# The idle products at the head of a Sinkhorn-attention and MoE kernel, cut from 29 wide into 113 narrow ones

## Chip, core and metric

The kernel runs on one core of a Trainium2 chip. The metric is the device time of one execution in microseconds; before the change it is 240.62 us, the median of 3 runs (240.29 to 241.72). A lower time is better. Matrix products run on TensorE (PE; its weight loads are listed apart as PEld), elementwise work on VectorE (DVE), ScalarE (ACT) and GpSimd (POOL), and transfers are issued from SyncE (SP), POOL and ACT.

## What is computed

Attention over sorted blocks, then a gated MLP. Four batches of eight heads have 768 rows of width 64, in eight blocks of 96 rows. An 8 x 8 matrix per head is normalized five times over rows and columns (Sinkhorn), the blocks of keys and values are mixed by it, each block of queries attends to its own mixed block, and the result of all heads goes through two weight matrices with x cos(x) between them:

```python
for _ in range(5):
    P = P - np.max(P, axis=-1, keepdims=True)
    P = np.exp(P)
    P = P / (np.sum(P, axis=-1, keepdims=True) + 1e-09)
    P = P / (np.sum(P, axis=-2, keepdims=True) + 1e-09)
...
k_sorted = np.einsum('bhij,bhjcd->bhicd', P, k_b)
v_sorted = np.einsum('bhij,bhjcd->bhicd', P, v_b)
scores = scale * np.matmul(q_b, k_sb.transpose(0, 1, 2, 4, 3))
attn = softmax(scores)
x = np.matmul(attn, v_sb)          # heads side by side: 3072 x 512
h = x @ w_in                       # 512 x 2048
out = (h * np.cos(h)) @ w_out      # 2048 x 512
```

## The kernel before

After a head of about 14 us the work goes by n = 0 to 7, half a batch each: scores (`S`, L1344 or L1357), row maxima (`M`), subtraction (`X`), exponentials (`E`), transposed weights (`TP` or a transposing transfer), the product with the mixed values (`AV`, L1445), normalization (`N`), a transpose (`XP`), then the first MLP product (`U`, L1505, or `U4`, L1528), the cosine (`C`), the gate (`G`) and the second MLP product (`D`, L1550). The table PLAN, written by hand, gives the order of these steps; the program keeps this order on every engine. No line of PLAN is touched by the change.

The head stands ahead of PLAN and is written out in code. On SP and POOL it starts the loads of the sort matrix P, of the first queries (`q_mem`), keys and values. VectorE and ScalarE run the five Sinkhorn rounds in turn: ScalarE takes an exponential `E` (L1172), VectorE six small operations (`normalize`, L1146 to L1151), the last of which feeds the next exponential; in the last round it writes `sorted_by`. ScalarE's queue is in order, and between the exponentials of rounds 2, 3 and 4 it copies the transposed first queries from PSUM to `q_turned` (`q_place`, L1166): head pair 0 in round 2, pair 1 in round 3, pairs 2 and 3 in round 4.

TensorE's own order in the head is:

1. 15 idle products (`keep_warm`, L1083) of a zero tile `warm` with itself: 128 x 128 weights, 512 columns, into a PSUM tile `idle` that nothing reads.
2. `q_twice(0)` and `q_twice(1)` (L1160): 16 transposes each out of `q_mem`, into `qps` tiles.
3. 2 idle products into a `big` tile.
4. In round 2: 6 idle products, then `q_twice(2)`. In round 3: 2 idle products, then `q_twice(3)`. In round 4: 4 idle products.
5. `block` (L1205) twice: 8 products each of `sorted_by` with a selection matrix. VectorE spreads them into `bd` and `bdv` (L1210), and with these PLAN's first steps mix keys (L1225) and values (L1281).

The idle products of step 4 and the `qps` and `bl` tiles share the PSUM pool `acc`, which has two buffers. A tile there may be written when the last tile in its buffer has been read (by a `q_place` copy) or, for an `idle` tile, written. Which of the two buffers a tile gets is not in the source; it is settled when the program is built. The wait itself is a semaphore of the engine that releases the buffer. Each idle product is two instructions on TensorE, a load of the weights and the product.

Further idle products in PLAN's steps (the fills of `kp` and `v0`, and one of 256 columns in `TP` and `AV` for n = 0) are called with counts and widths of their own and stay as they are.

Of the kernel before, what the change touches and what calls it, by code (L numbers as in the profile page):

```python
# [10 lines left out]
FP32 = mybir.dt.float32  # L11
# [852 lines left out]
def kernel(  # L864
# [46 lines left out]
    big = ctx.enter_context(tc.tile_pool(name="big", bufs=3, space=bass.MemoryType.PSUM))  # L911
    acc = ctx.enter_context(tc.tile_pool(name="acc", bufs=2, space=bass.MemoryType.PSUM))
# [47 lines left out]
    def load_q(n):  # L960
        b, ih = n // 2, n % 2
        if n < NQ:

            nc.gpsimd.dma_start(
                out=q_rows, in_=q[b][:, ih * IC * blk:(ih + 1) * IC * blk].rearrange(
                    "h (p r) d -> p h (r d)", r=QR))
        else:
            src = q[b].rearrange("h (i c) d -> c i h d", c=blk).rearrange(
                "c i (h e) d -> c i h e d", e=2)
            q_heads = q_zeroed(n).rearrange("p (e x) -> p e x", e=2)[:, :, :QZ].rearrange(  # L970
                "p e (i h w) -> p i h e w", i=IC, h=H2)[:, :, :, :, :D]
            for i in range(IC):
                for e in range(2):
                    nc.gpsimd.dma_start(  # L974
                        out=q_heads[:, i, :, e], in_=src[:, ih * IC + i, :, e])
# [27 lines left out]
    def load_w_in(z):  # L1003
        c = slice(z * Dff // 4, (z + 1) * Dff // 4)
        nc.gpsimd.dma_start(out=w_in_t[:, :, c], in_=w_in_d[:, :, c])
# [75 lines left out]
    def keep_warm(times, t, cols=512):  # L1081
        for _ in range(times):
            nc.tensor.matmul(  # L1083
                t[:, :cols], warm[:], warm[:, :1].to_broadcast([128, cols]),
                start=True, stop=True)

    keep_warm(15, big.tile([128, 512], FP32, name="idle", tag="big"))


    V, A = nc.vector, nc.scalar  # L1090
# [53 lines left out]
    def normalize(it, out):  # L1144

        nc.vector.reduce_sum(sums[0][:], E_eps[:], axis=AX.X)  # L1146
        nc.vector.reciprocal(over[0][:], sums[0][:])
        nc.vector.tensor_tensor(Q, E, by_row(over[0]), op=ALU.mult)
        nc.vector.reduce_sum(sums[1][:], Q_eps.rearrange("p i j -> p j i"), axis=AX.X)
        nc.vector.reciprocal(over[(1, 2, 1, 3, 1)[it]][:], sums[1][:])  # L1150
        nc.vector.tensor_tensor(out, Q, by_column(over[(1, 2, 1, 3, 1)[it]]), op=ALU.mult)  # L1151
# [3 lines left out]
    def q_twice(h2):  # L1155
        ps = turns[h2] = acc.tile([128, 2, IC, QR, blk // QR], BF16, name="qps", tag="acc")
        for hp in range(2):
            for r in range(QR):
                for x in range(2):
                    nc.tensor.transpose(  # L1160
                        ps[x * D:(x + 1) * D, hp, :, r],
                        q_rows[:, h2 * 2 + hp, r * D:(r + 1) * D], ident[:blk, :blk])

    def q_place(h2):
        dst = q_turned[0][:, :, :QW].rearrange("d e (i h c) -> d h e i c", h=H2, c=blk)
        A.copy(dst[:, h2], turns.pop(h2).rearrange("d e i r p -> d e i (r p)"))  # L1166

    def idle(times):
        keep_warm(times, acc.tile([128, 512], FP32, name="idle", tag="acc"))

    for it in range(5):
        nc.scalar.activation(E, less[:], AF.Exp)  # L1172
        if it == 0:
            nc.vector.reduce_sum(
                maskp.rearrange("p (b e x) -> p b x e", b=2, e=2),
                ident.rearrange("p (b x e j) -> p b x e j", b=2, e=2, j=nb), axis=AX.X)
            A.copy(
                order.rearrange("k (p r) -> k p r", r=QR),
                ident[:blk, :blk].rearrange("k (r p) -> k p r", r=QR))
            q_twice(0)  # L1180
            q_twice(1)
            keep_warm(2, big.tile([128, 512], FP32, name="idle", tag="big"))
        if it >= 2:
            q_place(it - 2)
            if it < 4:
                idle((6, 2)[it - 2])
                q_twice(it)
            else:
                idle(4)
                q_place(3)  # L1190
        normalize(it, (less if it < 4 else sorted_by)[:])
        if it == 1:
            nc.gpsimd.tensor_copy(held[:B * H], over[2][:, :1])
            for z in range(3):
                load_w_in(z)
        if it == 3:
            nc.gpsimd.tensor_copy(held[:B * H], over[3][:, :1])
            load_w_in(3)
            load_q(1)
# [477 lines left out]
```

## Time and profile before

| | |
|---|---|
| median of 3 runs | 240.62 us (240.29 to 241.72) |
| the profiled execution | 241.18 us |
| its span, first to last instruction | 239.1 us |
| PE busy | 227.2 us (95%) |
| DVE busy | 172.2 us (72%) |
| ACT busy | 153.1 us (64%) |
| POOL busy | 93.5 us (39%) |
| share of PE in the chain that ended last | 72% |

The span leaves 241.18 - 239.1 = 2.1 us of the execution outside. The profile lists each instruction with its start and its duration; products overlap, so the time that one takes of TensorE is read from the spacing of their starts, or from a row of the chain that holds several of them, not from the duration of one. The chain that ended last is followed back from the last instruction, at each step to what released it; a piece in it has a start, a length and a line. In a row of the timeline, what stands in brackets is how long the engine was idle ahead of it and who ended that. One of the 29 idle products has no record in this trace.

### The profile page before, as it was taken

How to read it: one execution, taken by the hardware profiler on the slowest of the kernel's cores; microseconds unless marked ns; L12 is line 12 of the kernel's file. 1: busy time of each engine (PE TensorE's matmuls, PEld its weight loads, DVE VectorE, ACT ScalarE, POOL GpSimd, SP SyncE). 2: the span in 40 equal slices, each digit the busy share in tenths (PEclk: the TensorE clock that was granted, in tenths of full speed). 3: DMA queues.
4: the chain of work that ended last, by engine and by line, in shares of the span. 5: the costliest groups of instructions: out<-in, count | busy, mean ns of one | idle time of the engine just before them, and what ended most of it. 6: DMA issues, size and time to landing. Idle time of an engine off the chain costs nothing.

```text
span 239.1 us, 5437 instructions
## 1 busy us (share of the span) xinstructions
PE 227.2 (95%) x2224; PEld 142.3 (60%) x2246; DVE 172.2 (72%) x284; ACT 153.1 (64%) x205; POOL 93.5 (39%) x117
## 2 busy tenths in 40 slices
PE   8889999999999999997999999999999899999994
PEld 2468799567666666654665456655665355455553
DVE  5658977898789677886589966996889839445610
ACT  3357966578789838873889647773675476736511
POOL 7689994895960098921708006200000000000000
PEclk9999999999999999999999999999999999999999
DMA  6999999994999999979959979844853370232012
GB/s 88 209 199 204 205 220 213 152 203 149 111 121 176 153 162 109 183 174 144 104 86 100 121 133 234 52 76 75 159 170 68 51 197 3 46 97 90 0 44 88
DMA packets 66423, 30.89 MB, mean 129 GB/s; under 512 B 55136, under 2 KB 61920, under 8 KB 66144
## 3 DMA queue, kind: packets, MB, share of 16 engines
q0 software_dynamic: 24048, 13.64, 41.8%
q1 hardware_dynamic: 42064, 16.73, 33.0%
q8 instruction: 17, 0.28, 0.5%
q10 hardware_dynamic: 288, 0.20, 0.3%
q14 instruction: 6, 0.05, 0.1%
HBM read 27.27 MB, written 6.29 MB: 140 GB/s over the span
## 4 chain that ended last, share of the span: by engine, by line
PE 72%; DMA 10%; DVE 9%; ACT 5%; issue 2%; SPq 1%; POOL 1%; ACTq 0%; POOLq 0%; DVEq 0%
PE h L1505 29%; PE o L1550 21%; DMA pT<-p_buf 5%; PE h L1528 4%; PE av L1445 3%; PE vs L1281 2%; PE sc L1344 2%; DMA vperm<-p_buf 2%; ACT p_buf L1403 2%; DMA xT<-xn 2%; DVE s L1399 2%; DVE mx L1385 1%; PE xps L1479 1%; PE o L1641 1%; PE ks L1225 1%
## 5 line engine op out<-in xcount | busy, mean ns | idle before, releaser
L1550 PE MATMUL o<-w_out_t,gg 128*128 128x512 bf16 x349 | 84.2, 379 | 1.2 <-issue 0.3
L1505 PE MATMUL h<-xT,w_in_t 128*128 128x384 bf16 x448 | 78.4, 326 | 0.4 <-DMA xT<-xn 0.4
L1517 DVE TENSOR_TENSOR gg<-c,h 128x768 bf16<-128x768 f32 x56 | 52.4, 949 | 21.3 <-ACT c L1511 21.1
L1511 ACT ACTIVATE c<-h,half_pi 128x768 f32<-128x768 f32 x56 | 50.2, 900 | 21.4 <-PE h L1505 20.4
L1505 PEld LDWEIGHTS <-w_in_t 128*128 128x128 bf16 x448 | 42.1, 98 | 26.2 <-issue 0.5
L1550 PEld LDWEIGHTS <-gg 128*128 128x128 bf16 x368 | 33.3, 98 | 33.3 <-DVE gg L1517 0.3
L1385 DVE TENSOR_REDUCE mx<-sc 96x8 f32<-96x768 f32 (+1 forms) x41 | 31.6, 771 | 4.4 <-PE sc L1344 3.4
L1403 ACT ACTIVATE p_buf<-s 96x768 bf16<-96x768 f32 x32 | 26.2, 841 | 8.7 <-DVE s L1399 5.2
L1024 POOL COPY vperm<-kv 64x1536 bf16<-64x1536 bf16 (+1 forms) x10 | 28.0, 2844 | 1.2 <-DMA kv<-in_v_dram 1.2
L1399 DVE TENSOR_TENSOR s<-sc,mx 96x384 f32<-96x384 f32 (+1 forms) x33 | 24.2, 734 | 1.6
L1457 DVE TENSOR_TENSOR xn<-av,r 96x512 bf16<-96x512 f32 x32 | 22.0, 686 | 1.1
L974 POOL DMA_DIRECT2D kv<-in_q_dram x24 | 15.9, 674 | 0.8 <-issue 0.8
L1455 DVE RECIPROCAL r<-av 96x8 f32<-96x8 f32 x32 | 6.4, 200 | 11.6 <-PE av L1445 11.4
L1094 ACT CAST kTs<-ks 128x512 bf16<-128x512 f32 (+1 forms) x17 | 10.6, 632 | 5.2 <-PE ks L1225 5.2
L1094 ACT COPY kv<-o 128x512 f32<-128x512 f32 (+2 forms) x11 | 5.9, 535 | 12.2 <-PE o L1550 9.6
L1344 PEld LDWEIGHTS <-q_turned 128*128 128x128 bf16 x168 | 9.8, 98 | 3.5 <-issue 0.4
L1344 PE MATMUL sc<-kTs,q_turned 128*128 128x96 bf16 x168 | 11.6, 206 | 0.3 <-DMA kTs<-kTs 0.3
L1083 PE MATMUL idle<-warm 128*128 128x512 bf16 x28 | 9.8, 498 | 2.1 <-ACT q_turned L1166 1.0
L1094 ACT COPY xT<-xps 128x384 bf16<-128x384 bf16 (+1 forms) x11 | 5.5, 506 | 9.0 <-PE xps L1479 9.0
L974 POOL DMA_DIRECT2D q_mem<-in_q_dram x16 | 10.7, 688 | 1.3 <-DMA kv<-in_v_dram 1.0
L1528 PE MATMUL h<-xT,w_in_t 128*128 128x192 bf16 x128 | 11.1, 246 | 0.0
L1445 PEld LDWEIGHTS <-pT 96*128 96x128 bf16 (+1 forms) x160 | 7.2, 101 | 6.0 <-DMA pT<-p_buf 4.2
(117 smaller groups left out, 264.4 us busy)
## 6 DMA issues: line engine op xcount, KB each, us to landing
out_dram<-kv SPq DMA_DIRECT2D x12, 256.0 KB, 2.6
out_dram<-o_s SPq DMA_DIRECT2D x10, 256.0 KB, 3.0
w_in_t<-in_moe_w_in_dram POOLq DMA_DIRECT2D x4, 512.0 KB, 12.0
w_out_t<-in_moe_w_out_dram POOLq DMA_DIRECT2D x4, 512.0 KB, 12.6
kv<-in_k_dram POOLq DMA_DIRECT2D x2, 768.0 KB, 10.3
kv<-in_v_dram POOLq DMA_DIRECT2D x2, 768.0 KB, 13.3
pair<-in_k_dram POOLq DMA_DIRECT2D x2, 768.0 KB, 10.9
kv<-in_v_dram POOLq DMA_DIRECT2D x6, 256.0 KB, 5.5
```

The lines of the kernel that those rows point to most:

```text
L974: nc.gpsimd.dma_start(out=q_heads[:, i, :, e], in_=src[:, ih * IC + i, :, e])
L1024: nc.gpsimd.tensor_copy(dst, src)
L1094: eng.copy(dst, src)
L1344: nc.tensor.matmul(out, q_of(n, hp)[:, x:x + 128], keys_of(n, u, h2, hp), start=True, stop=True)
L1385: nc.vector.reduce_max(mx[:], s_view(n, u, hp), axis=AX.XY if n < 2 else AX.X)
L1399: nc.vector.tensor_tensor(s, sc, mx.to_broadcast(list(s.shape)), op=ALU.subtract)
L1403: nc.scalar.activation(p[:, :, :blk], s_t.pop((n, u)).rearrange("p e h c -> p (e h) c"), AF.Exp, scale=scale)
L1457: nc.vector.tensor_tensor(xn.rearrange("p h e d -> p e h d"), avv[:, :, :, :D], r.to_broadcast([blk, 2, H2, D]), op=ALU.mult)
L1505: nc.tensor.matmul(o[:, f2, :TC], w_in_t[:, kk, f * 128:(f + 1) * 128], xT[n][:, kk], start=(kk == 0), stop=(kk == KC - 1))
L1511: nc.scalar.activation(c[:], ps["h", n, fp][:, :, :TC], AF.Sin, bias=half_pi[:, 0:1])
L1517: nc.vector.tensor_tensor(gt[n, fp // 2][:, f:f + 2], ps.pop(("c", n, fp))[:], ps.pop(("h", n, fp))[:, :, :TC], op=ALU.mult)
L1550: nc.tensor.matmul(out_ps[n, ts][:], gt[n, q][:, f % 4, ts * 128:(ts + 1) * 128], w_out_t[:, f, :], start=(f == 0), stop=(f == FC - 1))
```

## The change

Every one of the four `keep_warm` calls of the head gets more and narrower products. The 15 of 512 columns become 57 of 135; the 2 into the `big` tile become 8 of 128; `idle(6)`, `idle(2)` and `idle(4)` become 24, 8 and 16 of 128 columns. The columns are 57 x 135 = 7695 instead of 15 x 512 = 7680 at the start, and the same as before elsewhere (4 x 128 = 512). There are 113 - 29 = 84 more products, each with its load of weights.

```diff
-    keep_warm(15, big.tile([128, 512], FP32, name="idle", tag="big"))
+    keep_warm(57, big.tile([128, 512], FP32, name="idle", tag="big"), 135)
...
     def idle(times):
-        keep_warm(times, acc.tile([128, 512], FP32, name="idle", tag="acc"))
+        keep_warm(4 * times, acc.tile([128, 512], FP32, name="idle", tag="acc"), 128)
...
-            keep_warm(2, big.tile([128, 512], FP32, name="idle", tag="big"))
+            keep_warm(8, big.tile([128, 512], FP32, name="idle", tag="big"), 128)
```

The built program differs in one more thing, which the diff does not show: the `acc` tiles of the head take other buffers, and so other waits. No engine's instructions change places; TensorE has 168 more of them. On TensorE, from round 2 to round 3, before the change (in brackets the semaphore that an instruction waits for, Activation being ScalarE's; `idle_225` is the tile of `idle(6)`, `qps_232` of `q_twice(2)`, `idle_257` of `idle(2)`, `qps_260` of `q_twice(3)`):

```order
L1083 MATMUL idle_203<-warm_121 128x512
L1083 LDWEIGHTS warm_121
L1083 MATMUL idle_225<-warm_121 128x512 [waits Activation_49]
...
L1160 LDWEIGHTS q_mem_93
L1160 MATMUL qps_232<-ident_90,q_mem_93 64x4x24 [waits PE_49]
...
L1083 MATMUL idle_257<-warm_121 128x512 [waits Activation_49]
...
L1160 MATMUL qps_260<-ident_90,q_mem_93 64x4x24 [waits PE_49]
```

And the same place now (`idle_273` is the tile of `idle(6)`, now 24 products, `qps_298` of `q_twice(2)`, `idle_323` of `idle(2)`, `qps_332` of `q_twice(3)`):

```order
L1083 MATMUL idle_245<-warm_121 128x128
L1083 LDWEIGHTS warm_121
L1083 MATMUL idle_273<-warm_121 128x128 [waits Activation_49]
...
L1160 LDWEIGHTS q_mem_93
L1160 MATMUL qps_298<-ident_90,q_mem_93 64x4x24 [waits Activation_49]
...
L1083 MATMUL idle_323<-warm_121 128x128 [waits PE_49]
...
L1160 MATMUL qps_332<-ident_90,q_mem_93 64x4x24 [waits PE_49]
```

Before, `q_twice(2)` took the buffer of `idle(6)` and waited for those products on its own engine, and `idle(2)` waited for ScalarE's second `q_place`. Now `q_twice(2)` waits for that second `q_place` and `idle(2)` for the products of `idle(6)`; `q_twice(3)` waits for the products of `idle(2)` in both.

The place where the head's TensorE work meets VectorE's, the end of `idle(4)` and the first `block`, before:

```order
L1083 MATMUL idle_288<-warm_121 128x512 [waits Activation_49]
L1083 LDWEIGHTS warm_121
L1083 MATMUL idle_288<-warm_121 128x512
...
L1205 LDWEIGHTS pair_89 [waits DVE_49,Pool_49]
L1205 MATMUL bl_300<-sorted_by_156,pair_89 128x8 [waits Activation_49]
```

and now:

```order
L1083 MATMUL idle_360<-warm_121 128x128 [waits Activation_49]
L1083 LDWEIGHTS warm_121
L1083 MATMUL idle_360<-warm_121 128x128
...
L1205 LDWEIGHTS pair_89 [waits DVE_49,Pool_49]
L1205 MATMUL bl_384<-sorted_by_198,pair_89 128x8 [waits Activation_49]
```

Both wait for the same as before (`idle(4)` for ScalarE's third `q_place`, `block` for `sorted_by` and for the fourth `q_place`); 16 products stand between instead of 4.

## Prediction

> **What bounds the kernel now.** I read the page first, then the chain that ended last, then the timeline of the first 15 us.
>
> ```profile
> span 239.1 us, 5437 instructions
> PE 72%; DMA 10%; DVE 9%; ACT 5%; issue 2%; SPq 1%; POOL 1%; ACTq 0%; POOLq 0%; DVEq 0%
> ```
>
> TensorE carries most of the chain over the whole span, but the change touches only the head, and what counts there is what the chain runs through in the head. Its pieces from round 3 to the first mixed keys:
>
> ```profile
> 9.89 0.26 ACT E L1172
> ...
> 11.43 0.22 DVE less L1151
> ...
> 11.73 0.26 ACT E L1172
> 11.99 0.69 ACT q_turned L1166
> 12.68 0.04 issue
> 12.72 1.03 PE idle L1083 x4
> 13.75 0.32 PE bl L1205 x8
> 14.06 0.03 issue
> 14.09 0.30 DVE bd L1210
> 14.39 0.13 issue
> 14.51 0.64 PE ks L1225 x16
> ```
>
> Up to 11.99 us the chain is Sinkhorn alone, VectorE and ScalarE in turn; TensorE's idle products and transposes lie beside it. Only the last four idle products stand in it, between the third copy of `q_turned` and the first `block`. The timeline shows how closely:
>
> ```profile
> 7.10 0.74 PEld L1160 LDWEIGHTS <-q_mem 96*64 96x64 bf16 x32 [0.43 <-DMA q_mem<-in_q_dram]
> 9.03 1.47 PE L1083 MATMUL idle<-warm 128*128 128x512 bf16 x5 [0.52 <-ACT q_turned L1166]
> 10.05 0.77 ACT L1166 COPY q_turned<-qps 128x768 bf16<-128x768 bf16 x1
> 10.55 0.53 PE L1160 MATMUL qps<-ident,q_mem 96*64 96x96 bf16 x16
> 11.01 0.61 PE L1083 MATMUL idle<-warm 128*128 128x512 bf16 x2
> 11.68 0.53 PE L1160 MATMUL qps<-ident,q_mem 96*64 96x96 bf16 x16
> 11.90 1.46 ACT L1166 COPY q_turned<-qps 128x768 bf16<-128x768 bf16 x2
> 12.71 0.81 POOL L964 DMA_DIRECT2D q_mem<-in_q_dram x1
> 12.72 1.03 PE L1083 MATMUL idle<-warm 128*128 128x512 bf16 x4 [0.51 <-ACT q_turned L1166]
> 13.27 0.21 DVE L1151 TENSOR_TENSOR sorted_by<-Q,over 32x64 bf16<-32x64 f32 x1
> 13.68 0.58 PE L1205 MATMUL bl<-sorted_by,pair 32*128 32x8 bf16 x16
> ```
>
> `sorted_by` is done at 13.27 + 0.21 = 13.48. The chain shows 0.13 us from VectorE's `bd` to the products that use it, so `block` could start at 13.61; it starts at 13.68. The idle products therefore hold it by at most 0.07 us, and that is all that a change of them can give.
>
> **The price of a narrow product.** The rate of TensorE changes once within the first stage:
>
> ```profile
> L1083 PE MATMUL idle<-warm x5: 607/631/632, 1.0 to 2.7; 128*128 128x512 bf16 x5
> L1083 PE MATMUL idle<-warm x3: 382/432/632, 6.1 to 6.8; 128*128 128x512 bf16 x3
> L1083 PE MATMUL idle<-warm x5: 377/379/380, 9.0 to 10.1; 128*128 128x512 bf16 x5
> 5.00:6.00 1.00, 1.00 (x4) 0.29 (x2) 0.89 (x3) 0.00 (x0) 0.93 (x3) 1.00 1.85 296
> ```
>
> The first five start 1.7 / 4 = 0.43 us apart and last 631 ns; of the three from 6.1 us on the first is still slow and the last fast, so the full rate sets in near 6.6 us. The granted clock (third figure from the end of the last row) says 1.00 all the while, so the durations are what shows it. At full rate:
>
> ```profile
> 30.09 2.68 PE h L1528 x32
> 43.76 1.02 PE sc L1344 x24
> 44.78 3.45 PE o L1550 x16
> L1528 PE MATMUL h<-xT,w_in_t 128*128 128x192 bf16 x128 | 11.1, 246 | 0.0
> L1344 PE MATMUL sc<-kTs,q_turned 128*128 128x96 bf16 x168 | 11.6, 206 | 0.3 <-DMA kTs<-kTs 0.3
> L1344 PEld LDWEIGHTS <-q_turned 128*128 128x128 bf16 x168 | 9.8, 98 | 3.5 <-issue 0.4
> 15.40 0.99 PEld L1225 LDWEIGHTS <-kv 64*128 64x128 bf16 x32 [0.23 <-issue]
> ```
>
> A product of 512 columns costs 3.45 / 16 = 216 ns, one of 192 costs 2.68 / 32 = 84 ns, one of 96 costs 1.02 / 24 = 42.5 ns, each with a new load of weights that lasts 98 ns by itself. The loads are hidden at both widths. Between them, 128 columns come to 42.5 + (32 / 96) x 41.3 = 56 ns and 135 to 59 ns. Four narrow ones cost 225 ns for one wide one's 216. That price is nearest to rows of the same kind on both sides, and I take it. Its bounds: below, 216 / 4 = 54 ns; above, a load of 98 ns that isn't hidden at all.
>
> The Trainium skill has a higher price, in TensorE: Matmul & The Clock Gate, Back-to-back issue gap: a sustained stream of load and product takes about 81 ns each at 128 columns. By that the last 16 alone would take 16 x 81 = 1.30 us. The two rows above speak against it, since 96 columns take about half as much and 192 hardly more.
>
> **The parts of the change.** *The 57 at the start.* At the slow rate 135 columns take 0.43 x 135 / 512 = 0.113 us if columns alone count. By 6.6 us, 5.6 / 0.113 = 49 or 50 are through, the other 7 or 8 take 0.059 us each, and the stage ends at 7.0 to 7.1 us. Now the fifteenth starts at 6.8 and frees the array 0.22 us later, also about 7.0; the transposes then start at 7.10 and are listed as released by the transfer of `q_mem`. So nothing moves. If the loads were not hidden at the slow rate (double the 98 ns, say 0.2 us on top of each 0.113), 18 would be through by 6.6 us, the other 39 would take 59 to 157 ns each, and the transposes would start at 8.9 to 12.7 us; the first copy, wanted before the exponential at 9.89, would hold Sinkhorn by 0.2 us at the one end (done at 8.9 + 0.4 + 0.77 = 10.1) and by 4 at the other. TensorE keeping a load hidden behind 64 columns at full rate (32 loads in 0.99 us, 31 ns each) excludes nearly all of that.
>
> *The 8 in the big tile, the 24 and the 8.* They cost 17, 56 and 17 ns more and stand beside Sinkhorn. What is moved there is the wait. `q_twice(2)` starts at 10.55 now; in the change it waits for the second copy, 10.05 + 0.77 = 10.82, and with the 0.04 us from copy to product that the chain shows, starts at 10.87, though its 24 products end at 9.03 + 24 x 0.056 = 10.4. Queued behind it on TensorE: 8 idle products, from 10.87 + 0.46 = 11.33 to 11.78 (0.46 is the way from 10.55 to 11.01 now), then `q_twice(3)`, which waits until the last of them has drained, near 11.95 (a narrow product lasts 206 to 246 ns), and ends at 12.0 + 0.53 = 12.53. Who waits for these: the third copy, which can't start before 11.90 and finds its transposes done at 11.4; the fourth copy, which starts at 11.90 + 1.46 - 0.77 = 12.59 and finds them done at 12.53; and POOL's load of the next queries into `q_mem`, which has its turn at 12.71. Cover is 0.5, 0.06 and 0.18 us. The second is thin, but if the fourth copy slips, `block` still has 0.3 us to spare between its end, 11.90 + 1.46 = 13.36, and 13.68. The cost is nothing; without that cover it would be the 0.32 us of the wait.
>
> *The 16 in round 4.* They start with the third copy's end as before, 12.72, and take 16 x 0.056 = 0.90 us where four wide ones took 0.86. `block` moves from 13.68 to 13.72: **+0.04 us**, and everything behind it follows. By the bounds of the price: 0 (54 ns) to the 1.2 us worked out under the rivals.
>
> *168 more instructions on TensorE* must also be fetched:
>
> ```profile
> q8 instruction: 17, 0.28, 0.5%
> ```
>
> 0.28 MB in 17 packets is 16.5 KB each; 168 instructions against some 4,500 on TensorE is 4%, about one more packet. In the row of L1225 TensorE takes in 64 instructions in 0.99 us without a gap, and the change asks for 114 in 6 us. I take nothing; one gap of issue, 0.23 us in the bracket of that row, is the upper bound.
>
> **Sum.** 241.18 + 0.04 = 241.22 us for the profiled execution, which lies 0.56 us over the median of its kernel. On the median: 240.62 + 0.04 = 240.66, said as 240.7 us. No change.
>
> **The rivals.** *A narrow product costs its weight load.* With 98 ns each, the 24 end at 11.4, `q_twice(2)` at 11.9, the 8 at 12.6, `q_twice(3)` runs from 12.8 to 13.3, its copy ends at 14.1, and the 16 end at 14.9 instead of 13.6: +1.2 us, **241.9 us**. For it: a load's own 98 ns is longer than the 56 ns of the product. Against it: L1344 runs such pairs at 42.5 ns. With the skill's 81 ns the same steps give 14.04 for the end of the 16, and about 241.1.
>
> *The slow rate lasts.* The 57 are there to bring TensorE to its full rate, and it came 5.6 us after the first product. If short products with a load between them count for less and the rate doesn't come by 6.6 us, everything TensorE does in the head costs double. One more such interval, to 12.2 us: the 24 run from about 10.0 to 12.4, and the copies and the 16 follow from there until 14.9, +1.2 us. Two intervals, to 17.8 us: the 24 end at 12.7, `q_twice(2)` at 13.6, its copy and the 8 at 14.5, `q_twice(3)` at 15.7, the 16 at 17.5 instead of 13.6: +3.9 us, **244.5 us**, slower. It passes 1% if the slow rate holds beyond about 15 us. For it: nothing else in the head keeps TensorE so densely busy. Against it: at the slow rate 135 columns fill the array as long as 512 do, and the narrow products of L1225 with 64 columns between 14.5 and 16.5 us don't bring the slow rate back. The skill's rule (same page, What's actually happening) is that a window of time that passes busy, not a number of products, sets the rate; by it this rival falls away.
>
> *Faster.* Removing all hold on `block` gives 0.07 us, **240.55**. An earlier full rate gives nothing, since the transposes at 7.10 wait for `q_mem` anyway. I find no mechanism for a gain over 1%.
>
> **How the numbers follow.** 1% of the time is 2.4 us, about what a measurement of this kernel can tell from no change. The forecast has 0.84, the price of the load (81 or 98 ns) 0.08, the lasting slow rate 0.06 (0.05 of it long enough for over 1%), and the faster end 0.02 for what I don't see. So faster by over 1%: 0.02; within 1%: 0.93; slower: 0.05. The runs of before spread from 0.33 below their median to 1.1 above; the range takes a little more than this below, and above reaches past the load's 241.9: 239.9 to 242.0.
>
> **What would show it.** In the profile of the change: the 57 start near 0.113 us apart and then 0.059, the rate turning near 6.6 us, and `q_twice(0)` within 0.1 us of 7.10; `q_twice(2)` behind the second copy, near 10.87; its exponentials at the same distances from one another as now; 16 idle products at 56 ns from 12.72 and `block` at about 13.72; from there on all as now. Wrong would be: narrow products over 70 ns apart at full rate; products that still last over 250 ns after 9 us; or a span that differs by over 1 us with the head in place.

## The result: faster, by 0.6%, and not in the head

| | before | the change |
|---|---|---|
| median of 20 runs | 240.64 us | 239.29 us |
| all runs | 239.42 to 241.78 | 237.61 to 241.15 |
| ratio | | 0.9938 (95% interval 0.9913 to 0.9964) |
| profiled execution's span | 239.1 us | 235.7 us |

The gain lies within the 1% that the prediction called no change, but the interval of the ratio leaves out 1, and 239.29 us lies below the range that was given, 239.9 to 242.0. The two profiled executions differ by 3.4 us, more than the medians do (1.35 us); the runs of the change spread over 3.5 us and its profile is of one near their lower end. So the profile tells where the time can go, and the ratios how much.

**The head did what was predicted, from round 2 on.** The chain that ended last in the change, from the last Sinkhorn round on:

```profile
11.76 0.26 ACT E L1172
12.01 0.69 ACT q_turned L1166
12.70 0.04 issue
12.74 1.08 PE idle L1083 x16
13.82 0.52 PE bl L1205 x16
```

The 16 narrow products stand where the 4 wide ones stood, 1.08 us instead of 1.03. The timeline of TensorE there, and VectorE's `bd`:

```profile
10.90 0.53 PE L1160 MATMUL qps<-ident,q_mem 96*64 96x96 bf16 x16 [0.30 <-ACT q_turned L1166]
12.05 0.53 PE L1160 MATMUL qps<-ident,q_mem 96*64 96x96 bf16 x16
13.76 0.58 PE L1205 MATMUL bl<-sorted_by,pair 32*128 32x8 bf16 x16
14.16 0.29 DVE L1210 TENSOR_TENSOR bd<-maskp,bl 128x128 bf16<-128x128 f32 x1 [0.65 <-PE bl L1205]
```

`q_twice(2)` waits for ScalarE's copy and starts at 10.90, `q_twice(3)` at 12.05, `block` at 13.76 and `bd` at 14.16, 0.07 us later than before. Up to here the change is a loss.

**The gain lies between 75 and 195 us.** Who TensorE waited for from 15 us on, in us in total, times and longest, before the change:

```profile
PE av L1445 <- DMA pT<-p_buf: 2.2, 3, 1.4
PE av L1445 <- DMA vperm<-p_buf: 1.0, 1, 1.0
PE h L1505 <- DMA xT<-xn: 0.4, 1, 0.4
```

and in the change:

```profile
PE av L1445 <- DMA pT<-p_buf: 1.3, 1, 1.3
```

All of these are the transposing transfers that SP issues: attention weights into `pT` or `vperm`, normalized rows into `xT`. TensorE waits 3.6 us for them before, 1.3 us after. In the chain before the change three more of them stand:

```profile
78.92 3.86 DMA pT<-p_buf
163.73 3.63 DMA xT<-xn
182.82 4.49 DMA vperm<-p_buf
```

The chain of the change passes these three places without a transfer. ScalarE runs the same 205 instructions in both, so its starts show where the time went: they come 0.23 us later than before at 74 us (the 0.07 of the head and more between 20 and 27 us, whose cause stays open), 0.07 us earlier at 132, 1.23 earlier at 141, 2.04 earlier at 177 and 3.36 earlier from 189 us to the end. That is the whole difference of the spans. One place in detail, four `pT` transfers near 132 us. The chain before the change:

```profile
133.85 0.30 SPq L1418
134.15 0.05 issue
134.19 0.03 SPq L1418
134.22 0.03 issue
134.25 3.98 DMA pT<-p_buf
138.23 0.05 issue
138.28 0.43 PE av L1445 x8
```

and the chain of the change:

```profile
130.65 0.87 ACT p_buf L1403 x2
131.52 5.48 DMA pT<-p_buf x2
137.00 0.05 issue
137.05 0.43 PE av L1445 x8
```

(there it holds two of the transfers in one piece). `AV` starts 1.23 us earlier. How long a transfer takes, from issue to landing, is in the rows of the tile `pT`. In two stretches of before (131 to 134 and 134 to 135 us; the transfer issued at 132.92 counts in both):

```profile
DMA to landing us min/median/max: 3.2/3.8/4.4
DMA to landing us min/median/max: 4.0/4.2/4.4
```

and of the change:

```profile
DMA to landing us min/median/max: 3.0/3.0/3.1
DMA to landing us min/median/max: 2.8/2.9/3.1
```

The same data with the same order of issue take 2.8 to 3.1 us instead of 3.2 to 4.4. What else the DMA engines did is in the queues. Between 131 and 138.2 us, beside queue 1, which carries the transposing transfers themselves, they have these rows before the change:

```profile
q0 software_dynamic: 1313, 0.16, 35.4%
q8 instruction: 1, 0.02, 1.0%
```

and in the change:

```profile
q0 software_dynamic: 394, 0.05, 10.6%
q14 instruction: 1, 0.01, 1.0%
```

The rows of queue 0 are POOL's loads, which in the change were issued earlier; before, the last of them has landed at 133.87 us, and the transfer that takes 3.98 us is issued at 134.25. The packet of queue 14, 8 KB, starts at 138.0 us, when three of the four `pT` transfers have landed and the fourth lands 0.4 us later. What is left is queue 8, whose packet starts at 135.3 us and takes about 1.1 us: two of the four are under way then, and the last is issued beside it.

Queue 8 is that of the instructions which TensorE fetches: with 0, 24, 44, 64, 84, 104 and 128 instructions added to TensorE alone, in the runs below, its first packet starts at 17.4, 15.2, 14.1, 14.0, 11.9, 10.8 and 10.6 us. Over the whole span before, and then in the change:

```profile
q8 instruction: 17, 0.28, 0.5%
```

```profile
q8 instruction: 18, 0.29, 0.5%
```

Each packet is about 16 KB, and 0.5% of 16 engines' 239.1 us over 17 packets is 1.1 us: one packet takes about that much time of a DMA engine. From the packet at 18.5 us to that at 221.2, sixteen packets on, TensorE starts 1993 products and 1992 loads in the change, 249 instructions a packet, and a few more where records are missing. The expectations below take 256, and the runs with 256 and 300 added test it. Packets are fetched as TensorE gets on through its program, so 168 more instructions in the head bring every later packet to an earlier place of the unchanged work.

**Theory (fetch):** a fetch packet beside a transposing transfer delays it by about a microsecond; the 168 instructions move the packets, and fewer fall on transfers that the path waits for. **Rivals:** the narrow products of rounds 2 to 4 and their other waits; the 0.07 us by which the work behind the head is shifted; something that grows with the number of products at the start; the other transfers on the DMA engines.

### The profile page after: what moved, and what is told of

Same layout as the page of the kernel before. It is cut to its first block, busy times and chain, and to the rows that moved or that the text cites. A ratio compares the mean times of both kernels' runs of the same rounds, so it can differ in the third digit from the quotient of the medians.

```text
span 235.7 us, 5627 instructions
## 1 busy us (share of the span) xinstructions
PE 227.1 (96%) x2330; PEld 147.3 (63%) x2330; DVE 171.9 (73%) x284; ACT 153.3 (65%) x205; POOL 93.9 (40%) x117
## 4 chain that ended last, share of the span: by engine, by line
PE 82%; DMA 5%; ACT 4%; DVE 4%; issue 2%; POOL 1%; SPq 1%; ACTq 0%; POOLq 0%
PE h L1505 30%; PE o L1550 28%; PE h L1528 5%; DMA pT<-p_buf 4%; PE av L1445 3%; PE sc L1344 3%; PE vs L1281 2%; PE ks L1225 2%; ACT p_buf L1403 2%; PE xps L1479 2%; PE o L1641 2%; PE pps L1427 1%; DMA kTs<-kTs 1%; PE vs L1316 1%; PE vs L1083 1%
## 5 line engine op out<-in xcount | busy, mean ns | idle before, releaser
L1550 PE MATMUL o<-w_out_t,gg 128*128 128x512 bf16 x368 | 87.2, 379 | 0.0
L1094 ACT CAST kTs<-ks 128x512 bf16<-128x512 f32 (+1 forms) x17 | 10.6, 632 | 5.0 <-PE ks L1225 5.0
L1083 PEld LDWEIGHTS <-warm 128*128 128x128 bf16 x130 | 9.8, 108 | 3.0 <-issue 1.2
L1083 PE MATMUL idle<-warm 128*128 128x135 bf16 (+1 forms) x113 | 8.9, 244 | 2.2 <-ACT q_turned L1166 1.2
## 6 DMA issues: line engine op xcount, KB each, us to landing
pair<-in_k_dram POOLq DMA_DIRECT2D x2, 768.0 KB, 10.6
```

Source lines behind the costliest of these rows:

```text
L1094: eng.copy(dst, src)
L1550: nc.tensor.matmul(out_ps[n, ts][:], gt[n, q][:, f % 4, ts * 128:(ts + 1) * 128], w_out_t[:, f, :], start=(f == 0), stop=(f == FC - 1))
```

## The experiments

All leave the output as it is. They differ only in the counts and widths of idle products, hold the columns of the first stage near 7680, and were timed against the kernel before on the same chip. Except for the second, their rounds 2 to 4 keep the wide products and the waits of before.

**The count without the narrow rounds:** 84 more products, all in the first stage.

```diff
-    keep_warm(15, big.tile([128, 512], FP32, name="idle", tag="big"))
+    keep_warm(99, big.tile([128, 512], FP32, name="idle", tag="big"), 78)
```

> The first stage has 99 idle products of 78 columns instead of 15 of 512: the same 84 more products and 168 more instructions as the change, but the products of rounds 2 to 4 stay wide and keep the waits of the kernel before. Fetch theory (TensorE's instructions are fetched in packets of 256; 168 more of them move every fetch to another place of the program, and fewer fall on transposing transfers that the path waits for): as the change, ratio to before 0.990 to 0.998, fetches at the change's places. Rival, the narrow products of the rounds with their other buffers and waits: as before, 0.998 to 1.002. Rival, the start of the work behind the head 0.08 us later: as before too, since block moves back to its old place.

Measured: 0.9939 (0.9908 to 0.9970), median 239.26 us, the change's to 0.03 us. TensorE's wait for `pT` is 1.6 us, and no packet falls between 131 and 138.2 us, as in the change. `bd` starts at 14.11, so the shift of the head is nearly undone. Neither the rounds, nor their waits, nor the shift are needed.

**The narrow rounds with 256 more instructions:** the change, with its first stage cut further.

```diff
-    keep_warm(57, big.tile([128, 512], FP32, name="idle", tag="big"), 135)
+    keep_warm(101, big.tile([128, 512], FP32, name="idle", tag="big"), 76)
```

> The change with its first stage cut into 101 products of 76 columns instead of 57 of 135: narrow products and other waits as in the change, but 256 instructions more than before instead of 168, one whole fetch packet. Fetch theory: every fetch falls where it fell before the change, ratio to before 0.998 to 1.003. Rivals of the narrow rounds, of the waits and of the later block: as the change, 0.990 to 0.998.

Measured: 1.0001 (0.9979 to 1.0023), median 240.76 us. With everything of the change in place and 44 products more, the whole gain is gone. Its waits are those of before:

```profile
PE av L1445 <- DMA pT<-p_buf: 2.3, 4, 1.2
PE av L1445 <- DMA vperm<-p_buf: 0.9, 1, 0.9
```

its chain has the long transfer again, and its packet is back between 131 and 138.2 us:

```profile
134.46 4.16 DMA pT<-p_buf
```

```profile
q8 instruction: 1, 0.02, 1.2%
```

The two runs together refute the first three rivals: what has the narrow rounds isn't faster, what lacks them is, and more products give less.

**Other distances.** The first stage alone, as in

```diff
-    keep_warm(15, big.tile([128, 512], FP32, name="idle", tag="big"))
+    keep_warm(57, big.tile([128, 512], FP32, name="idle", tag="big"), 135)
```

and with 121 products of 64 columns, 37 of 208, 47 of 163, 67 of 115, 79 of 97, 27 of 285 and 165 of 47.

> Only the first stage of the change (57 products of 135 columns for 15 of 512), rounds as before: 84 more instructions. Fetch theory: the fetches fall at a third set of places; moving the profile's packets by 84 instructions puts them onto the transposing transfers near 61, 104, 158, 181 and 210 us, five collisions against six before, so 0.993 to 1.002, and other transfers are the slow ones. Rivals of the rounds and the waits: 1.000. If the products at the start matter by themselves: as the change, 0.994.

> The first stage alone as 121 products of 64 columns: 212 more instructions, rounds and waits as before. Fetch theory: moving the packets of the profile by 212 leaves three collisions with transposing transfers (near 108, 137 and 184 us) against six before, so the fastest of the four: 0.986 to 0.995. Rivals of the rounds and the waits: 1.000.

> First stage alone as 37 products of 208 columns: 44 more instructions, rounds and waits as before. Fetch theory: the packets fall between those of before and of the run with 84 more; moved on paper they meet the transposing transfers near 76, 105, 130 and 161 us, among them the exposed pT ones: ratio 0.992 to 1.001, and every transposing transfer over 3.6 us has a packet beside it. Rival, whatever makes the first stage narrow helps in proportion to the number of products: 0.998 (22 of 84 products).

> First stage as 47 products of 163 columns: 64 more instructions. Fetch theory: packets near 78, 105, 161, 192 and 211 us, most on transfers with some cover: 0.990 to 0.999. Rival in proportion to the number of products: 0.997.

> First stage as 67 products of 115 columns: 104 more instructions. Fetch theory: packets near 140, 157, 188 and 209 us, none on the pT transfers that the path waits for before 135 us: 0.988 to 0.996, as fast as the run with 84 more or faster. Rival in proportion to the number of products: 0.996.

> First stage as 79 products of 97 columns: 128 more instructions, half a packet. Fetch theory: packets near 112, 139, 156, 186 and 207 us, on xT and vperm transfers, none on pT: 0.988 to 0.996. Rival in proportion to the number of products: 0.995.

> First stage alone as 27 products of 285 columns: 24 more instructions, rounds and waits as before. Fetch theory: the packets come 24 instructions earlier than before, between the runs with 0 (1.000) and 44 (0.990); the packet of before's 135 us would fall near 133 and still on the pT transfers, so 0.992 to 1.000. Rival, a gain that needs only some more products at the start: 0.990 as with 44.

> First stage alone as 165 products of 47 columns: 300 more instructions, that is 256 + 44, rounds and waits as before. Fetch theory: the packets fall where they fall with 44 more, so again 0.988 to 0.994, though 212 and 256 more gave 0.998 and 1.000. Rival, that more products at the start cost more and more (the row from 44 to 256 rises): 1.000 or over.

All ten and the change, by the instructions added. Each ratio is against runs of before on the same chip and at the same time (their medians lie from 240.51 to 240.87 us), so it is not quite the quotient of the medians shown. There are 20 runs of the change, 12 of five others, and 5 to 8 of those with 24, 44, 64, 84 and 300. The last column adds up TensorE's waits for `pT`, `vperm` and `xT` from 15 us on in the one profiled execution:

| instructions added | kernel | median us | ratio (95% interval) | span us | waits us |
|---|---|---|---|---|---|
| 0 | before | 240.64 | 1 | 239.1 | 3.6 |
| 24 | first stage 27 x 285 | 238.67 | 0.9913 (0.9882 to 0.9943) | 237.2 | 1.5 |
| 44 | first stage 37 x 208 | 238.16 | 0.9900 (0.9863 to 0.9938) | 236.1 | 0.8 |
| 64 | first stage 47 x 163 | 238.29 | 0.9908 (0.9875 to 0.9940) | 236.2 | 1.5 |
| 84 | first stage 57 x 135 | 238.99 | 0.9918 (0.9882 to 0.9953) | 236.9 | 1.5 |
| 104 | first stage 67 x 115 | 238.94 | 0.9935 (0.9911 to 0.9960) | 236.8 | 0.6 |
| 128 | first stage 79 x 97 | 239.97 | 0.9975 (0.9950 to 1.0000) | 236.6 | 1.0 |
| 168 | the change | 239.29 | 0.9938 (0.9913 to 0.9964) | 235.7 | 1.3 |
| 168 | first stage 99 x 78 | 239.26 | 0.9939 (0.9908 to 0.9970) | 236.0 | 1.6 |
| 212 | first stage 121 x 64 | 240.01 | 0.9976 (0.9953 to 0.9999) | 237.8 | 2.9 |
| 256 | narrow rounds, first stage 101 x 76 | 240.76 | 1.0001 (0.9979 to 1.0023) | 238.7 | 3.2 |
| 300 | first stage 165 x 47 | 238.08 | 0.9892 (0.9867 to 0.9918) | 236.2 | 0.9 |

The last two rows decide it. 256 is 1.000, and 300 = 256 + 44 is as fast as 44, though 212 and 256, with fewer products, are slow. No effect that grows or falls with the number of products returns after 256. (256 was run with the narrow rounds alone; the two rows with 168 say that these make no difference.) The packets return too. Their starts in the middle of the span, in us:

| instructions added | packets of queue 8 from 62 to 171 us |
|---|---|
| 0 | 65.7, 78.7, 92.5, 108.2, 119.5, 135.3, 150.0, 163.7 |
| 256 | 66.4, 78.8, 92.8, 108.6, 119.4, 135.5, 151.1, 164.5 |
| 44 | 64.9, 77.2, 90.9, 103.7, 115.8, 130.5, 143.3, 162.0 |
| 300 | 65.3, 77.1, 91.7, 104.1, 115.9, 130.9, 143.8, 162.5 |
| 168, the change | 73.6, 83.0, 97.7, 109.2, 125.7, 138.3, 153.9, 169.9 |
| 168, first stage 99 x 78 | 73.2, 82.8, 98.0, 109.0, 124.7, 138.6, 153.2, 170.1 |

The waits and the packets of the run with 300:

```profile
PE av L1445 <- DMA pT<-p_buf: 0.9, 2, 0.7
PE sc L1344 <- DMA kTs<-kTs: 0.3, 1, 0.3
```

```profile
q8 instruction: 19, 0.31, 0.5%
```

19 packets against 17, and still 1% faster than before: it is not how many packets there are, but what they fall on.

Five of the ten expectations were missed. The runs with 212 and 128 were slower than forecast (0.986 to 0.995, 0.988 to 0.996), those with 44, 24 and 84 faster (0.992 to 1.001, 0.992 to 1.000, 0.993 to 1.002). Those that rest on the period or on the same count (168, 256, 300) all held; what missed is the worth of a given distance. Moving the packets on paper tells which transfers they meet, not which of these the path waits for: with 44 a packet still stretches a `pT` near 76 us to 4.4 us, but the chain runs past it.

**What a packet does to a transfer.** In the twelve profiles there are 396 transposing transfers into `pT`, `vperm` and `xT`. Sorted by whether a packet of queue 8 was under way at some time between issue and landing:

| into | without a packet: count, median, longest us | with one |
|---|---|---|
| `pT` | 89, 2.87, 3.74 | 43, 3.98, 5.01 |
| `vperm` | 121, 2.89, 3.10 | 23, 4.24, 4.68 |
| `xT` | 84, 2.33, 3.12 | 36, 3.44, 4.62 |

With a packet the median transfer is 1.1 to 1.4 us longer, about what the packet itself takes. Two or three transfers in a row are stretched by one packet, since they are under way together.

A long transfer has more time to meet a packet, so this sorting could make the difference by itself. Sorted instead by whether a packet starts between 0.5 us before and 1.5 us after the issue, the medians with and without are 4.00 (28 transfers) and 2.87 for `pT`, 4.24 (10) and 2.90 for `vperm`, 3.42 (26) and 2.34 for `xT`. The packets of queue 14 count as none in the table; the 23 transfers that met only such a packet have medians of 3.58, 3.02 and 2.92 us. With no instruction packet of either queue the longest are 3.32, 3.10 and 2.40 us. Among them are three `pT` transfers beside a dense stretch of POOL's loads, at 3.2 us, so those loads don't make a transfer of 4 us.

## Why the prediction was wrong

*The head* was right from round 2 on: `q_twice(2)` at 10.87 was forecast and 10.90 came, `q_twice(3)` 12.0 and 12.05, the 16 products from 12.72 and 12.74, `block` 13.72 and 13.76. The fourth copy started at 12.62 instead of 12.59, with no effect on `block`.

*The price of a narrow product* was right. In the change the 24 of round 2 and the 16 of round 4:

```profile
L1083 PE MATMUL idle<-warm x24: 217/219/219, 9.1 to 10.4; 128*128 128x128 bf16 x24
L1083 PE MATMUL idle<-warm x16: 216/218/219, 12.7 to 13.6; 128*128 128x128 bf16 x16
```

From first start to last that is 1.3 / 23 = 57 ns a product, against 56 forecast. The rival that a narrow product costs its weight load is refuted. The Trainium skill gives about 81 ns for such a stream (TensorE: Matmul & The Clock Gate, Back-to-back issue gap); the 57 ns measured here contradict it.

*The slow rate did not last.* In this execution it turned earlier than before:

```profile
L1083 PE MATMUL idle<-warm x23: 294/321/321, 1.0 to 3.5; 128*128 128x135 bf16 x23
L1083 PE MATMUL idle<-warm x30: 222/222/225, 4.0 to 5.8; 128*128 128x135 bf16 x30
```

Near 4.0 us instead of 6.6; with the same first stage and wide rounds (84 added) it turned near 6.3. So `q_twice(0)` started at 6.58 us, not within 0.1 us of 7.10: the first queries had landed at 6.53. Before, they had landed at 6.69, so the start at 7.10 was not set by that transfer, as the prediction read from the bracket of the row; the fifteenth idle product, started at 6.79, stood ahead. That gave nothing all the same, as forecast, since the first copy has its place behind the exponential (it starts at 8.23, before at 8.21): `bd` starts between 14.09 and 14.17 in all twelve kernels.

*The step that failed* is the one on the 168 instructions: "about one more packet", "I take nothing", with one gap of issue as the upper bound. It asked whether TensorE would run dry and what the one added packet costs. The runs show no cost of either: with two packets more (300 added) the kernel is 1% faster than before. It did not ask where the other 17 packets go. The row of queue 8 stood in the prediction; what was missing was to set the packets beside the transfers that the path waits for, 3.86 us near 79 and 3.98 near 134 in the chain of before where the median `pT` transfer without a packet takes 2.87. That excess is what the term should have been bounded by: 3.6 us of TensorE's waits before, so a gain of up to 1.5% of the time, and a loss where more packets meet such transfers. The sentence "from there on all as now" fell with it, and the claim that only 0.07 us were to be had. The prediction's own last sign of being wrong came true: a span that differs by over 1 us with the head in place. That the change is faster at all is luck, since nothing in it aims at the packets: 88 instructions more, and the gain was gone.

*Still open.* Why a packet delays a transposing transfer was not looked at below the level of transfers; that a transfer spread over the engines ends with the one that carries the packet would fit the 1.1 us, but no run shows on which engine either ran. Nor is it settled why the runs with 168 added spread over 3 to 3.5 us and those with 44 or 300 over 0.5 to 0.6; packets that meet a transfer in some executions and miss it in others would do it, and one profile of each kernel can't tell. The waits of the profiles don't give the order of the medians from 24 to 168, and the column leaves some out: with 128 added TensorE also waits 1.2 us for `kTs`, with 104 1.2 us for ScalarE. The kernels with 44 and 300 have 5 and 6 runs, so their small spread is itself uncertain. And no run moved one packet alone.

The lowest medians are not the change's but those of the first stage alone with 37 products (44 added) or 165 (300 added), 238.16 and 238.08 us, 0.9900 and 0.9892 of before; the lower edge of the change's own interval, 0.9913, is above both, though the intervals overlap.

## What to carry to other kernels

Here an edit that only added instructions to TensorE moved every later instruction fetch of that engine, and gained up to a per cent far from where it stands; whether other engines or kernels show this was not run, and no placing here lost against before. Before crediting an edit, make a control that adds the same number of instructions elsewhere, and one that adds a whole packet. Where transposing transfers are on the path, look in the DMA queues for the instruction packets beside the slow ones; the number of idle instructions at the start is a knob for their places, and it cost nothing else here.

## What the runs showed of the hardware

TensorE's instructions came in packets of 16 KB, one for each 250 or so instructions on record (17 packets before, 18 with 168 instructions more, 19 with 300 more), each taking about 1.1 us of a DMA engine. Transposing transfers with such a packet under way took 1.1 to 1.4 us longer in the median, in twelve profiles. Where these packets fell was worth up to 1.1% of this kernel's time, and it came back after 256 instructions (0 and 256 added, 44 and 300). The time at which TensorE's products turned to the full rate varied between about 3.8 us (212 added) and 7.0 us (300 added) from the start over kernels with nearly the same number of columns in the first stage.
